# Soft-MoE tail of an attention kernel: the seventh w2 whole in two pieces, two output tiles in column halves, idle matmuls in the waits for w2, the last w1 pair in one transfer

## The chip, the core and the metric

The kernel runs on one NeuronCore of a Trainium2 chip. Its five engines (TensorE for matmuls, VectorE, ScalarE, GpSimd, SyncE) run from queues of their own, and 16 DMA engines move data between the device memory and the core's on-chip memory. The metric is the device time of one launch in microseconds (us); lower is better. The time before is 180.16 us, the median of three runs.

## The reference

Attention over 8 batches of 8 heads, 576 positions and 64 values each: heads 0 to 3 see a window of 32 positions back, heads 4 to 7 see every fourth of the last 128. The result, as 4608 rows of 512, goes through a mixture of experts with soft slots: every expert has four slots, each a weighted mean of all rows; an expert is two matrices with a ReLU between; every output row is a weighted mean of the 32 slots' results.

```python
def _attn_ref(q, k, v):                     # q, k, v: (8, 8, 576, 64) float32
    scores = scale * np.matmul(q, k.transpose(0, 1, 3, 2))
    mask_plain = (rel >= 0) & (rel < window)
    mask_dil = (rel >= 0) & (rel < window * dilation) & (rel % dilation == 0)
    scores = np.where(masks[None, :, :, :], scores, -1000000000.0)
    ...                                     # softmax over the last axis
    return np.matmul(attn, v)

def _moe_ref(x, phi, w1, w2):               # x (4608, 512), phi (512, 32)
    logits = x @ phi                        # w1 (8, 512, 1024), w2 (8, 1024, 512)
    ...                                     # d: softmax of logits over the rows
    slot_input = (d.T @ x).reshape(E, S_per_e, D)
    for e in range(E):
        h = np.maximum(slot_input[e] @ w1[e], 0.0)
        slot_out[e] = h @ w2[e]
    ...                                     # c: softmax of logits over the slots
    return c @ slot_out.reshape(n_slots, D)
```

## The kernel before

**Inputs.** All inputs but a few first pieces are loaded by GpSimd's DMA queue, which turns float32 into float16 on the way. The order of that queue is written out by hand: q, k and v of the eight batches (`load_batch`, L180), then the experts' weights (`load_w1` L280, `load_both_w2` L292, `load_half` L298, `load_w2` L305). The batches live in eight "homes" of 8192 float16 values per partition, two to a tile (`twos`); when a batch has been used, its home takes one expert's w1 (4096 values per partition) and w2 (4096 values, 8 chunks of 512 columns). So a weight load waits until the attention has read what lay there. Batches in `PAIRED` (2 to 7) load the dilated heads' q and k (`qd`, `kd`) for two batches at once; `qp`, `kp` are those of the plain heads, `vp`, `vd` the two halves of v, and `vt` its last 64 rows.

**Attention.** A loop over 30 of the 32 units (batch, pair of heads), L676 to L730, computes scores, exponentials, values, the transposed rows and the slot weights. ScalarE, VectorE and TensorE work through it in program order; the weight loads are issued from within it: after unit 6 and 14 the first four experts', after unit 22 w1 of experts 4 and 5 and w2 of expert 4, at unit 26 w1 of expert 6, and after the loop w1 of expert 7, then w2 of experts 5, 6 and 7. The zeroing of four small tiles `hTp` stands in GpSimd's queue at units 26 to 29.

**Experts.** `expert_in` (L794) multiplies the slots by w1 for a pair of experts, `expert_turn` (L809) transposes the result, `expert_out` (L823) multiplies by w2, one matmul per chunk, all into one PSUM tile `sop`. `expert_out(e, side, chs)` can do one column half of the 512 (`SIDES`) and some of the chunks. The last two w2 come in pieces, in this order: chunks 0 to 3 of w2(6), the left column half of its chunks 4 to 7, the left half of w2(7) in chunks 0 to 5 and 6 to 7 (`PIECES`), and then the right halves of the same.

**Output.** When `sop`'s left half is complete it is copied to `so` (L895, ScalarE for the left, VectorE for the right), and the first `FIRST_TILES` = 3 of nine output tiles of 512 rows are computed for the left columns: `finish_rows` (L857) does a matmul for each of a tile's four row groups (L865), and ScalarE (L869) and VectorE (L871) take turns in scaling the result into `ot`; `finish_half` (L875) stores them from SyncE's queue (L881), tile 0 in two pieces, the others in one. The same follows for the right half, and then the other six tiles are done over all 512 columns (`finish_whole` L883, stores at L887, as grouped in `TOGETHER`). `warm` (L466) issues matmuls whose results nobody reads; at the start there are 12 of them.

Of the kernel before, what the change touches and what calls it, by code (L numbers as in the profile page):

```python
# [7 lines left out]
FP32 = mybir.dt.float32  # L8
# [6 lines left out]
H = 8  # L15
S = 576
D = 64
# [6 lines left out]
E_EXP = 8  # L24
# [6 lines left out]
RP, NP = 6, 96  # L31
RD = 24
# [5 lines left out]
NV = 2  # L38
SIDES = ((0, DMODEL // 2), (DMODEL // 2, DMODEL))
PIECES = ((0, 6), (6, 8))  # L40
HALF = 4
FIRST_TILES = 3
PAIRED = (2, 4, 6)
TOGETHER = ((3,), (4, 5), (6,), (7,), (8,))


@with_exitstack
def kernel(
# [10 lines left out]
    nc = tc.nc  # L59
# [13 lines left out]
    first = {}  # L73
# [106 lines left out]
    def load_batch(b):  # L180
        if b == 6:
            twos.append(big.tile([128, 2, 8192], FP16, name="home6", tag="home6"))
            homes.extend(twos[3][:, i] for i in range(2))
        t = homes[b]
        parts = raws.setdefault(b, {})
        at = 0

        def load_v(nm, h0, n_h, r0, dst):
            n_p = dst.shape[0]
            dst = dst.rearrange("p (h x) -> p h x", h=n_h)  # L190
            nc.gpsimd.dma_start(  # L191
                out=dst,
                in_=v[b, h0 : h0 + n_h, r0 : r0 + 4 * n_p, :].rearrange(
                    "h (p r) d -> p h (r d)", r=4
                ),
            )
            parts[nm] = dst.rearrange("p h (r d) -> p h r d", r=4)

        for nm, ten, hs, rows in (
            ("qp", q, 0, RP), ("kp", k, 0, RP), ("qd", q, 4, RD), ("kd", k, 4, RD),  # L200
        ):
            g = 4 * S // (NP * rows)
            n = g * rows * D
            if nm in ("qd", "kd") and b & 6 in PAIRED:
                if b % 2 == 0:
                    both = twos[b // 2][0:NP, :, at : at + n]
                    nc.gpsimd.dma_start(
                        out=both,
                        in_=ten[b : b + 2, hs : hs + 4].rearrange("e h s d -> e (h s) d").rearrange(
                            "e (p r) d -> p e (r d)", r=rows  # L210
                        ),
                    )
                    for i in range(2):
                        raws.setdefault(b + i, {})[nm] = both[:, i : i + 1]
                at += n
                continue
            parts[nm] = t[0:NP, at : at + n].rearrange("p (g x) -> p g x", g=g)
            at += n
            src = ten[b, hs : hs + 4].rearrange("h s d -> (h s) d").rearrange(
                "(g p r) d -> p g (r d)", g=g, r=rows  # L220
            )
            if b == 0 and nm in first:
                t0 = side_by_side(nm[0], 0)
                nc.vector.tensor_copy(
                    out=t0.rearrange("p r (h d) -> p r h d", h=2),
                    in_=first[nm].rearrange("p h (r d) -> p r h d", d=D),
                )
                nc.gpsimd.dma_start(out=parts[nm][:, 2:4], in_=src[:, 2:4])
            else:
                nc.gpsimd.dma_start(out=parts[nm], in_=src)  # L230
            if nm == "kp":
                if b == 0:
                    head_v = t[:, 6144:7168].rearrange("p (h x) -> p h x", h=4)
                    parts["vp"] = head_v.rearrange("p h (r d) -> p h r d", r=4)
                elif b < 2:
                    load_v("vp", 0, 4, 0, t[:, 6144:7168])
                else:
                    load_v("v", 0, 8, 0, t[:, 6144:8192])
                    parts["vp"], parts["vd"] = parts["v"][:, 0:4], parts["v"][:, 4:8]
                load_v("vt", 0, 8, 512, t[96:112, 0:2048])  # L240
        if b < 2:
            load_v("vd", 4, 4, 0, t[:, 7168:8192])

    def cast_first_v():
# [50 lines left out]
            in_=moe_w2[e : e + 2].rearrange("e (p c) f -> p e (c f)", p=128),  # L295
        )

    def load_half(e, side):  # L298
        d0, d1 = SIDES[side]
        nc.gpsimd.dma_start(  # L300
            out=w_tiles[e][1][:, HALF:8, d0:d1],
            in_=moe_w2[e].rearrange("(p c) f -> p c f", p=128)[:, HALF:8, d0:d1],
        )

    def load_w2(e):  # L305
        w2t = w_tiles[e][1]
        w2_from = moe_w2[e].rearrange("(p c) f -> p c f", p=128)
        if e == E_EXP - 2:
            nc.gpsimd.dma_start(
                out=w2t[:, 0:HALF].rearrange("p c f -> p (c f)"),  # L310
                in_=w2_from[:, 0:HALF].rearrange("p c f -> p (c f)"),
            )
            load_half(e, 0)
            return
        if e < E_EXP - 2:
            nc.gpsimd.dma_start(
                out=w2t.rearrange("p c f -> p (c f)"), in_=w2_from.rearrange("p c f -> p (c f)")
            )
            return
        w2t = w_tiles[e][1] = w2t.rearrange("p c f -> p (c f)").rearrange("p (s c f) -> p s c f", s=2, c=8)  # L320
        for n, (d0, d1) in enumerate(SIDES):
            if n == 1:
                load_half(e - 1, 1)
            for c0, c1 in PIECES:
                nc.gpsimd.dma_start(out=w2t[:, n, c0:c1], in_=w2_from[:, c0:c1, d0:d1])

# [318 lines left out]
            )  # L645
        nc.vector.tensor_copy(out=phi4, in_=pp[:, :, None, :].broadcast_to([128, 4, 4, N_SLOTS]))

    warm(12, heat)
    ctx.enter_context(tc.manual_schedule(engines={mybir.EngineType.Pool}))
    for b in range(B):  # L650
        load_batch(b)
# [24 lines left out]
    for u in range(NU - 2):  # L676
        b, ph = divmod(u, 4)
        if ph == 0:
            st = scores(u + 1)
            softmax_parts(u + 1, st)  # L680
            if u:
                x_transposes(u - 1)
            values(u)
        elif ph == 1:
            st = scores(u + 1)
            if b + 1 < B:
                regroup(4 * b + 4)
            if b:
                front_logits(b - 1)
            if b + 1 < B:  # L690
                transposes(4 * b + 4)
            values(u)
            x_transposes(u - 1)
            softmax_parts(u + 1, st)
        elif ph == 2:
            st = scores(u + 1)
            values(u)
            if b + 1 < B:
                regroup(4 * b + 6)
            softmax_parts(u + 1, st)  # L700
            if b + 1 < B:
                dilated_transposes(b + 1, "k")
                dilated_transposes(b + 1, "q")
            if b:
                front_rows(b - 1)
            x_transposes(u - 1)
            if u == 2:
                nc.vector.tensor_copy(out=vd[1][:, 0, 0:1], in_=xs[0][:, 0, 2 * D : 2 * D + 1])
        else:
            st = scores(u + 1)  # L710
            if b:
                front_slots(b - 1)
            values(u)
            softmax_parts(u + 1, st)
            if b + 1 < B:
                select_v(b + 1)
                transposes(4 * b + 6)
            x_transposes(u - 1)
            if b + 1 < B:
                spread_v(b + 1)  # L720
        if u in (6, 14):
            load_w1(u // 4 - 1, 2)
            load_both_w2(u // 4 - 1)
        if u == 22:
            load_w1(4, 2)
            load_w2(4)
        if u == 26:
            load_w1(6)
        if 26 <= u:
            nc.gpsimd.memset(hTp[u - 26], 0.0)  # L730

    load_w1(E_EXP - 1)
    load_w2(E_EXP - 3)
    load_w2(E_EXP - 2)
    load_w2(E_EXP - 1)
# [87 lines left out]
    def expert_out(e, side=None, chs=range(8)):  # L823
        d0, d1 = (0, DMODEL) if side is None else SIDES[side]
        w2t = w_tiles[e][1][:, side] if e == E_EXP - 1 else w_tiles[e][1][:, :, d0:d1]
        for ch in chs:
# [7 lines left out]
                skip_group_check=True,  # L834
            )

    expert_in(0)
    expert_in(1)
    for pr in range(4):
        expert_turn(pr)  # L840
        if pr < 2:
            expert_in(pr + 2)
        if pr == 1:
            front_sums(B - 1, ring.tile([128, 11, N_SLOTS], FP32, name="sums", tag="ring"))
        if pr < 3:
            expert_out(2 * pr)
            expert_out(2 * pr + 1)
    expert_out(6, chs=range(HALF))

    so = keep.tile([128, DMODEL], FP16, name="so", tag="so")  # L850
    fours = [
# [23 lines left out]
    def finish_half(i, side):  # L875
        d0, d1 = SIDES[side]
        ot = ots[i].rearrange("p j d -> p (j d)").rearrange("p (s j d) -> p s j d", s=2, j=4)[:, side]
        rows = out[512 * i : 512 * i + 512, d0:d1].rearrange("(m j) d -> m j d", j=4)
        for j0, j1 in ((0, 2), (2, 4)) if i == 0 else ((0, 4),):
            finish_rows(i, ot, range(j0, j1), d0, d1)  # L880
            nc.sync.dma_start(out=rows[:, j0:j1], in_=ot[:, j0:j1])  # L881

# [7 lines left out]
        )  # L890

    for n, (d0, d1) in enumerate(SIDES):
        expert_out(E_EXP - 2, n, range(HALF, 8))
        expert_out(E_EXP - 1, n)
        (nc.scalar.copy if n == 0 else nc.vector.tensor_copy)(out=so[:, d0:d1], in_=sop[:, d0:d1])  # L895
        for i in range(FIRST_TILES):
            finish_half(i, n)
# [36 lines left out]
```

## Time and profile before

| | |
|---|---|
| median of the runs (lowest to highest) | 180.16 us (179.79 to 180.61) |
| the profiled execution's own time | 180.08 us |
| its span, first to last instruction | 177.9 us |
| TensorE, VectorE, ScalarE, GpSimd busy | 145.3, 120.3, 124.0, 43.2 us |
| mean granted TensorE clock | 0.889 |
| DMA: GpSimd's queue / SyncE's queue | 30.41 MB / 10.26 MB |
| read from device memory, written to it | 61.93 MB, 9.44 MB |

In the lines of the profile, PE is TensorE, DVE VectorE, ACT ScalarE, POOL GpSimd and SP SyncE; L828 is line 828 of the kernel. A line of a timeline has the start, the time from the first start to the last end of a group, the engine, the line, the operation, what it writes and reads, the count, and in brackets the idle time before it and what ended that. A line of a table by stretches has the stretch, its length, the busy time and number of instructions of TensorE's matmuls, its weight loads, VectorE, ScalarE and GpSimd, then the granted clock (1.00 is full speed), the share of the 16 DMA engines' time that transfers in flight took (above 1 where they overlap), and GB/s. GB/s counts bytes as written, so a load that turns float32 into float16 counts half of what it reads.

### The profile page before, as it was taken

To read this page: it belongs to the slowest core of one execution; us is meant where nothing else is said; L and a number is where in the kernel's file an instruction comes from. 1 tells how busy PE (TensorE), PEld (TensorE's weight loads), DVE (VectorE), ACT (ScalarE), POOL (GpSimd) and SP (SyncE) were. 2 spreads that over 40 slices of the span, in tenths; PEclk is the share of its full clock that TensorE was granted. 3 is DMA by queue.
4 is the path that set the end of the run, shared out by engine and by line. 5 is a ranking of instruction groups with operands and counts; after the bars stand their busy time and mean duration, and the time that the engine had idled before them with its cause. 6 is when DMAs were issued, how large, how long until landed. Compare 5 with 4: busy or idle time off the path is not lost.

```text
span 177.9 us, 5105 instructions
## 1 busy us (share of the span) xinstructions
PE 145.3 (82%) x2137; PEld 99.4 (56%) x2137; DVE 120.3 (68%) x337; ACT 124.0 (70%) x233; POOL 43.2 (24%) x68
## 2 busy tenths in 40 slices
PE   6589889899999999999999999977899833897200
PEld 2367576687676676776677676755763311453000
DVE  7959896987988888898798898587120100689400
ACT  2588899999998998998998999952304100699300
POOL 7756443334333441001000500700011100000000
PEclk9987999999999999999999999996558985569955
DMA  5999999999999999999999999999999999999996
GB/s 162 243 198 207 199 205 212 199 200 204 212 200 201 202 213 199 217 223 214 214 219 215 215 217 217 214 219 214 214 221 214 208 197 194 252 382 423 431 424 267
DMA packets 27094, 41.28 MB, mean 232 GB/s; under 512 B 1344, under 2 KB 22848, under 8 KB 24512
## 3 DMA queue, kind: packets, MB, share of 16 engines
q0 software_dynamic: 22080, 30.41, 96.1%
q1 hardware_dynamic: 4784, 10.26, 14.9%
q10 hardware_dynamic: 208, 0.29, 0.6%
q8 instruction: 16, 0.26, 0.5%
q14 instruction: 6, 0.05, 0.1%
HBM read 61.93 MB, written 9.44 MB: 401 GB/s over the span
## 4 chain that ended last, share of the span: by engine, by line
DMA 47%; PE 31%; ACT 6%; DVE 5%; issue 2%; POOL 1%; DVEq 0%; ACTq 0%; POOLq 0%
DMA home<-in_moe_w_dram 37%; DMA home<-in_k_dram 9%; PE o L496 6%; PE f L865 4%; PE s L391 3%; PE rgx L516 3%; PE sel L270 2%; PE sel L259 2%; ACT kTd L364 2%; PE rgq L351 2%; ACT pd L424 2%; PE rgk L351 2%; PE l L534 1%; DVE ot L871 1%; ACT ot L869 1%
## 5 line engine op out<-in xcount | busy, mean ns | idle before, releaser
L501 DVE TENSOR_TENSOR x<-o,rc 128x640 f16<-128x640 f32 x32 | 26.6, 831 | 0.2
L417 ACT ACTIVATE pr<-s 128x960 f16<-128x960 f32 (+1 forms) x32 | 25.2, 795 | 0.0
L424 ACT ACTIVATE pd<-s 128x640 f16<-128x640 f32 x32 | 22.3, 719 | 1.1 <-PE s L400 1.0
L871 DVE TENSOR_SCALAR ot<-f,rrow 128x256 f32<-128x256 f32 (+1 forms) x24 | 13.2, 613 | 7.8 <-PE f L865 7.8
L433 DVE TENSOR_TENSOR Pp<-pr,fixed 128x1280 f16<-128x1280 f16 (+1 forms) x32 | 15.4, 520 | 0.0
L496 PE MATMUL o<-vd,P 128*128 128x65 f16 x256 | 15.1, 197 | 0.2 <-DVE x L501 0.2
L191 POOL DMA_DIRECT2D home<-in_v_dram x17 | 12.0, 709 | 13.1 <-DMA home<-in_k_dram 6.1
L869 ACT ACTIVATE ot<-f,rrow 128x256 f32<-128x256 f32 (+1 forms) x24 | 12.7, 583 | 2.6 <-PE f L865 2.2
L496 PE MATMUL o<-vp,Pp 128*128 128x65 f16 x288 | 13.7, 197 | 1.0 <-DVE x L501 1.0
L516 PE MATMUL rgx<-fixed,x 128*128 128x128 f16 x155 | 14.0, 222 | 0.6 <-ACT qTd L364 0.4
L865 PE MATMUL f<-so,ET 128*128 128x256 f16 (+1 forms) x48 | 12.3, 411 | 2.2 <-ACT ot L869 1.1
L286 POOL DMA_DIRECT2D home<-in_moe_w_dram x5 | 3.2, 637 | 41.5 <-PE sel L270 38.0
L352 ACT COPY qT<-rgq 128x576 f16<-128x576 f16 x16 | 10.3, 645 | 4.0 <-PE rgq L351 3.9
L391 PE MATMUL s<-qT,kTp 64*128 64x160 f16 (+1 forms) x160 | 10.6, 224 | 2.9 <-ACT pd L424 1.9
L534 PE MATMUL l<-xT,phi 128*128 128x288 f16 x64 | 11.6, 307 | 1.6 <-DVE xT L526 1.6
L496 PEld LDWEIGHTS <-P 128*128 128x128 f16 x288 | 11.8, 99 | 1.8 <-DVE xT L526 0.2
L522 ACT COPY xT<-rgx 128x512 f16<-128x512 f16 x16 | 9.7, 605 | 4.3 <-PE rgx L516 4.3
L496 PEld LDWEIGHTS <-Pp 128*128 128x128 f16 x288 | 11.1, 99 | 2.4 <-DVE x L501 1.2
L363 PEld LDWEIGHTS <-home 96*128 96x128 f16 x192 | 10.5, 100 | 3.1 <-DMA home<-in_k_dram 1.0
L391 PE MATMUL s<-qTd,kTd 64*128 64x144 f16 x128 | 12.1, 230 | 0.0
L443 DVE TENSOR_TENSOR P<-pd,fixed 128x1024 f16<-128x1024 f16 x16 | 10.9, 681 | 1.8 <-ACT pd L424 1.8
L516 PEld LDWEIGHTS <-x 128*128 128x128 f16 x160 | 10.2, 98 | 3.1 <-DVE x L501 1.6
(136 smaller groups left out, 318.3 us busy)
## 6 DMA issues: line engine op xcount, KB each, us to landing
home<-in_moe_w_dram POOLq DMA_DIRECT2D x5, 2048.0 KB, 38.9
home<-in_moe_w_dram POOLq DMA_DIRECT2D x4, 1024.0 KB, 33.9
out_dram<-ot SPq DMA_DIRECT2D x4, 1024.0 KB, 8.5
home<-in_v_dram POOLq DMA_DIRECT2D x6, 512.0 KB, 14.3
home<-in_q_dram POOLq DMA_DIRECT2D x9, 288.0 KB, 12.9
home<-in_k_dram POOLq DMA_DIRECT2D x9, 288.0 KB, 13.4
out_dram<-ot SPq DMA_DIRECT2D x4, 512.0 KB, 3.6
out_dram<-ot SPq DMA_DIRECT2D x1, 2048.0 KB, 6.8
```

What stands on the lines that cost most here:

```text
L191: nc.gpsimd.dma_start(out=dst, in_=v[b, h0 : h0 + n_h, r0 : r0 + 4 * n_p, :].rearrange("h (p r) d -> p h (r d)", r=4),)
L391: nc.tensor.matmul(st[:, g, at : at + n], kT[64 * g : 64 * g + 64, k0 : k0 + 128], qT[64 * g : 64 * g + 64, q0 : q0 + n], start=True, stop ...
L417: nc.scalar.activation(out=(pr[:, :, 0 : 3 * QW], pr[:, :, 3 * QW :])[part], in_=st[:, :, 0 : (480, 224)[part]], func=AF.Exp, scale=SCALE,)
L424: nc.scalar.activation(out=pr[:, part].rearrange("p c e t -> p e c t"), in_=st[:, :, 0 : 2 * DW].rearrange("p e (c t) -> p e c t", c=2), f ...
L433: nc.vector.tensor_tensor(out=Pp[:, :, b0 : b0 + nb, 0:w], in0=pr[:, :, b0 * QW : b0 * QW + nb * w].rearrange("p h (t c) -> p h t c", c=w) ...
L496: nc.tensor.matmul(ot[:, h, blk], lhs, rhs, start=(n == 0), stop=(n == len(mms) - 1), skip_group_check=True)
L501: nc.vector.tensor_tensor(out=xs[b][:, :, 2 * D * hp : 2 * D * hp + 2 * D].rearrange("p t (h d) -> p h t d", h=2), in0=ot[:, :, :, 0:D], i ...
L516: nc.tensor.transpose(rg[:, 128 * blk : 128 * blk + 128], x[:, blk, hl : hl + 128], ident)
L534: nc.tensor.matmul(lp, phi4[:, kc].rearrange("p a s -> p (a s)"), xT[:, kc, 288 * c : 288 * c + 288], start=(kc == 0), stop=(kc == 3), ski ...
L865: nc.tensor.matmul(fp, ET[:, c0 : c0 + 127 * nj + 1 : nj], so[:, d0:d1], start=True, stop=True)
L869: nc.scalar.activation(out=ot[:, j], in_=fp, func=AF.Copy, scale=scale)
L871: nc.vector.tensor_scalar(out=ot[:, j], in0=fp, scalar1=scale, scalar2=None, op0=ALU.mult)
```

## The change

- w2 of expert 6 is loaded in two pieces, chunks 0 to 3 and 4 to 7, each over all 512 columns; `load_half` is gone. w2 of expert 7 keeps its four pieces, which now follow each other. `expert_out(6)` takes its chunks before the column halves begin.
- Idle matmuls of 512 columns into a PSUM tile `idle`: 2 before `expert_out(5)`, 4 before the first chunks of expert 6, 4 after chunks 0 to 3 and 4 after chunks 4 to 7 (`FILL`).
- `FIRST_TILES` goes from 3 to 2; tile 2 is done whole. Tile 0 is stored in three pieces on the left side (row groups 0, 1, and 2 with 3) and in two on the right.
- w1 of experts 6 and 7 is one transfer, issued after the loop.
- Batches 2 to 7 lie otherwise in their two homes, and v of batches 4 and 5, and of 6 and 7, is one transfer each.
- 9 matmuls at the start in place of 12.

```diff
@@ -38,10 +38,10 @@
 NV = 2
 SIDES = ((0, DMODEL // 2), (DMODEL // 2, DMODEL))
 PIECES = ((0, 6), (6, 8))
-HALF = 4
-FIRST_TILES = 3
+FILL = (2, 4, 4, 4)
+FIRST_TILES = 2
 PAIRED = (2, 4, 6)
-TOGETHER = ((3,), (4, 5), (6,), (7,), (8,))
+TOGETHER = ((2,), (3,), (4, 5), (6,), (7,), (8,))
 
 
 @with_exitstack
@@ in load_batch
-        at = 0
+        paired = b & 6 in PAIRED
+        flat = twos[b // 2].rearrange("p e x -> p (e x)")
+        n = S * 4 * D // NP
...
+        at = (10240 + 2 * n * (b % 2)) if paired else 0
+        for nm, ten in (("qp", q), ("kp", k)):
+            home = flat if paired else t
+            parts[nm] = home[0:NP, at : at + n].rearrange("p (g x) -> p g x", g=4)
...
+        if paired:
+            if b < 4:
+                load_v("v", 0, H, 0, t[:, 6144:8192] if b == 2 else t[:, 0:2048])
+            elif b % 2 == 0:
+                load_v("v", 0, 2 * H, 0, flat[:, 6144:10240])
+            load_v("vt", 0, H, 512, t[96:112, 2048:4096])
+            parts["vp"], parts["vd"] = parts["v"][:, 0:4], parts["v"][:, 4:8]
+        else:
+            load_v("vt", 0, H, 512, t[96:112, 0:2048])
+        for i, (nm, ten) in enumerate((("qd", q), ("kd", k))):
...
+            elif b % 2 == 0:
+                both = flat[0:NP, 2 * n * i : 2 * n * i + 2 * n].rearrange("p (e x) -> p e x", e=2)
...
@@ in the loaders of w2, and below
             in_=moe_w2[e : e + 2].rearrange("e (p c) f -> p e (c f)", p=128),
         )
 
-    def load_half(e, side):
-        d0, d1 = SIDES[side]
-        nc.gpsimd.dma_start(
-            out=w_tiles[e][1][:, HALF:8, d0:d1],
-            in_=moe_w2[e].rearrange("(p c) f -> p c f", p=128)[:, HALF:8, d0:d1],
-        )
-
     def load_w2(e):
         w2t = w_tiles[e][1]
         w2_from = moe_w2[e].rearrange("(p c) f -> p c f", p=128)
-        if e == E_EXP - 2:
-            nc.gpsimd.dma_start(
-                out=w2t[:, 0:HALF].rearrange("p c f -> p (c f)"),
-                in_=w2_from[:, 0:HALF].rearrange("p c f -> p (c f)"),
-            )
-            load_half(e, 0)
-            return
-        if e < E_EXP - 2:
-            nc.gpsimd.dma_start(
-                out=w2t.rearrange("p c f -> p (c f)"), in_=w2_from.rearrange("p c f -> p (c f)")
-            )
+        if e < E_EXP - 1:
+            step = 4 if e == E_EXP - 2 else 8
+            for c in range(0, 8, step):
+                nc.gpsimd.dma_start(
+                    out=w2t[:, c : c + step].rearrange("p c f -> p (c f)"),
+                    in_=w2_from[:, c : c + step].rearrange("p c f -> p (c f)"),
+                )
             return
         w2t = w_tiles[e][1] = w2t.rearrange("p c f -> p (c f)").rearrange("p (s c f) -> p s c f", s=2, c=8)
         for n, (d0, d1) in enumerate(SIDES):
-            if n == 1:
-                load_half(e - 1, 1)
             for c0, c1 in PIECES:
                 nc.gpsimd.dma_start(out=w2t[:, n, c0:c1], in_=w2_from[:, c0:c1, d0:d1])
 
@@ -645,7 +644,7 @@
             )
         nc.vector.tensor_copy(out=phi4, in_=pp[:, :, None, :].broadcast_to([128, 4, 4, N_SLOTS]))
 
-    warm(12, heat)
+    warm(9, heat)
     ctx.enter_context(tc.manual_schedule(engines={mybir.EngineType.Pool}))
     for b in range(B):
         load_batch(b)
@@ -724,12 +723,10 @@
         if u == 22:
             load_w1(4, 2)
             load_w2(4)
-        if u == 26:
-            load_w1(6)
         if 26 <= u:
             nc.gpsimd.memset(hTp[u - 26], 0.0)
 
-    load_w1(E_EXP - 1)
+    load_w1(E_EXP - 2, 2)
     load_w2(E_EXP - 3)
     load_w2(E_EXP - 2)
     load_w2(E_EXP - 1)
@@ -834,6 +831,7 @@
                 skip_group_check=True,
             )
 
+    idle = ring.tile([128, 512], FP32, name="idle", tag="ring")
     expert_in(0)
     expert_in(1)
     for pr in range(4):
@@ -844,8 +842,13 @@
             front_sums(B - 1, ring.tile([128, 11, N_SLOTS], FP32, name="sums", tag="ring"))
         if pr < 3:
             expert_out(2 * pr)
+            if pr == 2:
+                warm(FILL[0], xT[:, 0, 0:512], idle)
             expert_out(2 * pr + 1)
-    expert_out(6, chs=range(HALF))
+    warm(FILL[1], xT[:, 0, 0:512], idle)
+    for n in range(2):
+        expert_out(6, chs=range(4 * n, 4 * n + 4))
+        warm(FILL[2 + n], xT[:, 0, 0:512], idle)
 
     so = keep.tile([128, DMODEL], FP16, name="so", tag="so")
     fours = [
@@ -876,7 +879,7 @@
         d0, d1 = SIDES[side]
         ot = ots[i].rearrange("p j d -> p (j d)").rearrange("p (s j d) -> p s j d", s=2, j=4)[:, side]
         rows = out[512 * i : 512 * i + 512, d0:d1].rearrange("(m j) d -> m j d", j=4)
-        for j0, j1 in ((0, 2), (2, 4)) if i == 0 else ((0, 4),):
+        for j0, j1 in (((0, 1), (1, 2), (2, 4)), ((0, 2), (2, 4)))[side] if i == 0 else ((0, 4),):
             finish_rows(i, ot, range(j0, j1), d0, d1)
             nc.sync.dma_start(out=rows[:, j0:j1], in_=ot[:, j0:j1])
 
@@ -890,7 +893,6 @@
         )
 
     for n, (d0, d1) in enumerate(SIDES):
-        expert_out(E_EXP - 2, n, range(HALF, 8))
         expert_out(E_EXP - 1, n)
         (nc.scalar.copy if n == 0 else nc.vector.tensor_copy)(out=so[:, d0:d1], in_=sop[:, d0:d1])
         for i in range(FIRST_TILES):
```

More of the change, by code (lines that the diff above doesn't have):

```diff
@@ L192, in load_v @@
                 out=dst,
-                in_=v[b, h0 : h0 + n_h, r0 : r0 + 4 * n_p, :].rearrange(
-                    "h (p r) d -> p h (r d)", r=4
-                ),
-            )
[L197 to L206, printed above, removed]
-                    nc.gpsimd.dma_start(
[L208 to L211, printed above, removed]
-                    )
[L213 to L217, printed above, removed]
+                in_=v.rearrange("b h s d -> (b h) s d")[
+                    H * b + h0 : H * b + h0 + n_h, r0 : r0 + 4 * n_p, :
+                ].rearrange("h (p r) d -> p h (r d)", r=4),
+            )
+            got = dst.rearrange("p h (r d) -> p h r d", r=4)
+            if n_h <= H:
+                parts[nm] = got
+            else:
+                for i in range(2):
+                    raws.setdefault(b + i, {})[nm] = got[:, H * i : H * i + H]
+        at = (10240 + 2 * n * (b % 2)) if paired else 0
+        for nm, ten in (("qp", q), ("kp", k)):
+            home = flat if paired else t
+            parts[nm] = home[0:NP, at : at + n].rearrange("p (g x) -> p g x", g=4)
             at += n
-            src = ten[b, hs : hs + 4].rearrange("h s d -> (h s) d").rearrange(
-                "(g p r) d -> p g (r d)", g=g, r=rows
-            )
-            if b == 0 and nm in first:
+            src = ten[b, 0:4].rearrange("h s d -> (h s) d").rearrange("(g p r) d -> p g (r d)", g=4, r=RP)
+            if b == 0:
                 t0 = side_by_side(nm[0], 0)
@@ L230, in load_batch @@
                 nc.gpsimd.dma_start(out=parts[nm], in_=src)
[L231 to L241, printed above, removed]
+        if b == 0:
+            head_v = t[:, 6144:7168].rearrange("p (h x) -> p h x", h=4)
+            parts["vp"] = head_v.rearrange("p h (r d) -> p h r d", r=4)
+        elif not paired:
+            load_v("vp", 0, 4, 0, t[:, 6144:7168])
+        if paired:
[5 more added lines that the diff above has]
+            parts["vp"], parts["vd"] = parts["v"][:, 0:4], parts["v"][:, 4:8]
+        else:
+            load_v("vt", 0, H, 512, t[96:112, 0:2048])
+        for i, (nm, ten) in enumerate((("qd", q), ("kd", k))):
+            if not paired:
+                at = 3072 + n * i
+                parts[nm] = t[0:NP, at : at + n][:, None, :]
+                nc.gpsimd.dma_start(
+                    out=t[0:NP, at : at + n],
+                    in_=ten[b, 4:8].rearrange("h s d -> (h s) d").rearrange("(p r) d -> p (r d)", r=RD),
+                )
+            elif b % 2 == 0:
+                both = flat[0:NP, 2 * n * i : 2 * n * i + 2 * n].rearrange("p (e x) -> p e x", e=2)
+                nc.gpsimd.dma_start(
+                    out=both,
+                    in_=ten[b : b + 2, 4:8].rearrange("e h s d -> e (h s) d").rearrange(
+                        "e (p r) d -> p e (r d)", r=RD
+                    ),
+                )
+                for j in range(2):
+                    raws.setdefault(b + j, {})[nm] = both[:, j : j + 1]
+        if not paired:
             load_v("vd", 4, 4, 0, t[:, 7168:8192])
@@ L307, in load_w2 @@
         w2_from = moe_w2[e].rearrange("(p c) f -> p c f", p=128)
-        if e == E_EXP - 2:
-            nc.gpsimd.dma_start(
-                out=w2t[:, 0:HALF].rearrange("p c f -> p (c f)"),
-                in_=w2_from[:, 0:HALF].rearrange("p c f -> p (c f)"),
-            )
-            load_half(e, 0)
-            return
-        if e < E_EXP - 2:
-            nc.gpsimd.dma_start(
-                out=w2t.rearrange("p c f -> p (c f)"), in_=w2_from.rearrange("p c f -> p (c f)")
-            )
+        if e < E_EXP - 1:
+            step = 4 if e == E_EXP - 2 else 8
+            for c in range(0, 8, step):
+                nc.gpsimd.dma_start(
+                    out=w2t[:, c : c + step].rearrange("p c f -> p (c f)"),
+                    in_=w2_from[:, c : c + step].rearrange("p c f -> p (c f)"),
+                )
             return
```

## The prediction

> **What bounds the kernel now.** I read the page's slices first, to see which resource never rests.
>
> ```profile
> PEclk9987999999999999999999999996558985569955
> DMA  5999999999999999999999999999999999999996
> GB/s 162 243 198 207 199 205 212 199 200 204 212 200 201 202 213 199 217 223 214 214 219 215 215 217 217 214 219 214 214 221 214 208 197 194 252 382 423 431 424 267
> ```
>
> The 16 DMA engines are busy from the first slice to the last: loads at about 200 to 220 GB/s (as written, after the cast) until some 150 us, then stores at 380 to 430. Compute runs alongside, so the time is the load stream, the seam between loads and stores, and the store stream. The clock falls to half around the seam.
>
> Next, GpSimd's timeline: does the load queue ever run dry?
>
> ```profile
> 97.60 0.54 POOL L286 DMA_DIRECT2D home<-in_moe_w_dram  x1 [12.67 <-PE sel L270]
> 111.57 0.53 POOL L286 DMA_DIRECT2D home<-in_moe_w_dram  x1 [11.23 <-PE sel L270]
> 124.28 0.70 POOL L325 DMA_DIRECT2D home<-in_moe_w_dram  x1 [8.92 <-DMA home<-in_moe_w_dram]
> 139.00 0.70 POOL L325 DMA_DIRECT2D home<-in_moe_w_dram  x1 [4.00 <-DMA home<-in_moe_w_dram]
> ```
>
> It does not. The w1 loads wait at 97.60 and 111.57 for a batch's last value selection, but with more than ten microseconds of transfers in flight. The L325 waits end when the transfer eight places ahead lands, which gives landing times: w1(4,5) 124.2, w2(4) 129.1, w1(6) 134.1, w1(7) 138.9.
>
> Then TensorE's timeline, whose DMA waits show when each late piece is there.
>
> ```profile
> 143.63 0.62 PE L828 MATMUL sop<-home,hTp 128*32 128x512 f16 x8 [1.22 <-DMA home<-in_moe_w_dram]
> 146.14 0.62 PE L828 MATMUL sop<-home,hTp 128*32 128x512 f16 x4 [1.55 <-DMA home<-in_moe_w_dram]
> 147.46 0.41 PE L828 MATMUL sop<-home,hTp 128*32 128x256 f16 x4 [0.71 <-DMA home<-in_moe_w_dram]
> 149.41 1.07 PE L828 MATMUL sop<-home,hTp 128*32 128x256 f16 x8 [1.54 <-DMA home<-in_moe_w_dram]
> 150.09 0.40 PE L828 MATMUL sop<-home,hTp 128*32 128x256 f16 x2
> ```
>
> w2(5) is there at 143.63, w2(6) chunks 0-3 (512 KB) at 146.14, the left half of chunks 4-7 (256 KB) at 147.46, and w2(7)'s left half at 149.41 (384 KB) and 150.09 (128 KB). So 512 KB whole costs 2.51 us, 256 KB in half rows 1.32, 384 KB 1.95, 128 KB 0.68. The right halves (256+384+128 KB) follow: 150.09 + 3.95 = 154.04.
>
> Last, quarter-microsecond stretches across the seam, and SP's queue.
>
> ```profile
> 150.75:151.00 0.25, 0.05 (x1) 0.05 (x1) 0.00 (x0) 0.15 (x1) 0.00 (x0) 0.50 1.45 193
> 152.25:152.50 0.25, 0.25 (x3) 0.19 (x2) 0.25 (x2) 0.25 (x2) 0.00 (x0) 0.50 0.82 111
> 153.25:153.50 0.25, 0.25 (x2) 0.00 (x0) 0.25 (x2) 0.25 (x2) 0.00 (x0) 0.50 1.23 293
> 154.50:154.75 0.25, 0.05 (x2) 0.00 (x0) 0.10 (x1) 0.00 (x0) 0.00 (x0) 0.50 0.67 238
> 161.50:161.75 0.25, 0.00 (x0) 0.00 (x0) 0.25 (x1) 0.25 (x2) 0.00 (x0) 1.00 1.56 615
> 152.15 0.91 SPq L881 DMA_DIRECT2D out_dram<-ot  x2
> ```
>
> The last column is GB/s. Loads taper from 193 to 111 after 151.2 (some engines are done before others) and end near 152.9, where stores begin: the first is issued at 152.15 and its bytes flow 0.8 us later. Column-half stores run at about 384 GB/s until 161.45, whole tiles at 427 until 176.2. A dip at 154.50 is the third store (tile 1's whole half, issued at 153.41 after four evictions).
>
> I model it from T = 151.80, the end of the first eviction (ACT, 151.36 + 0.44). Tile 1's half is stored by 156.0 = T + 4.2, set by evictions and SP's issues; four half tiles remain (2.10 MB / 384 = 5.46), then six whole ones (6.29 MB / 427 = 14.73). 156.0 + 5.46 + 14.73 = 176.2: the span's stores as seen.
>
> **The change, part by part.** All sums are against the profiled execution's 180.08 us (span 177.9, 2.2 around it), 0.08 under the median of 180.16.
>
> *w2(6) whole.* Chunks 4-7 come as one 512 KB piece before w2(7)'s left half. By the rows the left side is complete at 146.14 + 2.51 + 1.95 + 0.68 = 151.28 instead of 150.09: **+1.19**. The right side ends at 154.04 - (2 x 1.32 - 2.51) = 153.91. Every store waits for the left side, so this is on the path. What covers it? The taper ends at 152.9, the first store would be issued past that, and nothing queued takes its place.
>
> *Idle matmuls.* They sit in DMA waits. At full clock one more N=512 costs 0.22 us (late output matmuls: three in 0.95, four in 1.17), at half 0.43: the pair before expert 5 ends near 142.9, before 143.63; the next four lie beside the wait for 146.14; the others end near 147.4 and 149.9, before 148.65 and 150.60. If the clock holds, two isolated matmuls on the way to the first store (0.40 and 0.37 now) get about 0.12 us shorter each, estimated from half clock doubling the streaming of 256 columns. Does it hold? Three 3.4 us stretches that end at a change or none:
>
> ```profile
> 141.83:145.24 3.41, 1.53 (x20) 0.64 (x21) 0.26 (x2) 0.00 (x0) 0.00 (x0) 1.00 1.13 202
> 118.00:121.40 3.40, 1.88 (x41) 1.70 (x41) 2.54 (x5) 1.49 (x4) 0.00 (x0) 0.99 1.06 222
> 158.89:162.30 3.41, 2.65 (x12) 1.24 (x11) 3.41 (x6) 3.32 (x7) 0.00 (x0) 1.00 1.11 410
> ```
>
> The first column behind the length is TensorE's busy time. The clock fell after 45% and 55% busy and stayed after 78%. With the fills a 2.5 us period holds 0.4 + 0.9 us, about 52%: nearest to the rows that fell. Bounds -0.25 to 0; I take **-0.12**. The Trainium skill ("TensorE: Matmul & The Clock Gate", Part 1) says that half rate returns only after an idle window of about 3.4 us; by it the fills would hold the clock and the whole sum would be +0.59. The trace differs: no stretch at 121.4 or 145.24 was idle, and the clock fell.
>
> *Two tiles in halves.* Tile 2 (1.05 MB) moves from 384 to 427 GB/s: 2.73 - 2.46 = **-0.27**. The first whole store comes earlier in exchange: 160.25 - 154.04 = 6.21 us after the right side now, less four halves (4 x 0.22), so about 159.2 at half clock and 158.4 at full. Its bytes start 0.8 later, by 160.0; the halves run until T' + 4.2 + 2.73 = 159.9 or so. No gap, but little margin.
>
> *Finer first stores.* One row group is stored at a time for tile 0. Each issue takes SP about 0.4 us, so the four left stores are issued at T' + 0.14, 0.55, 1.0 and 1.6; tile 1's store still needs its evictions and stays at T + 4.2: 0. At best the bytes flow without a gap from T' + 1.0 (2.73 us): -0.46.
>
> *Merged loads.* Batches 5 and 7 bring no v of their own, w1(6,7) is one transfer. 512 KB took 2.51 us, half of w2(5)'s 4.87 is 2.44: 0.07 per transfer; w1(4,5), a pair, took 9.9, two singles 9.7: no gain. Between 0 and -0.28; **-0.08**.
>
> *Costs at nothing.* Three warm matmuls fewer (about 0.4 each), the new raw layout, and batch 4's qd and kd behind 512 KB more of v (2.5 us): hidden, since the experts start at 131.9 and run until they wait for weights at 138.76 and 143.63 (1.22). Without this cover each would shift the experts by its size. w1(6) is no longer issued at 97.60 but with w1(7) at about 112; w2(5) to w2(7) stand behind it on GpSimd's queue as they do now, the zeroing of hTp comes earlier, and w2(4) in flight until 129.1 covers 17 us. SP keeps 13 stores.
>
> Sum: 1.19 - 0.12 - 0.27 - 0.08 = **+0.72**: 180.80 by the profiled execution, 180.9 by the median.
>
> **Rivals.** *Slower: the clock falls inside the fills.* If it is at half from about 148.65, chunks 4-7 take 0.62 and four fills 4 x 0.43 = 1.7: TensorE is free at 150.97, past the landing at 150.60, which costs about 0.15. Whole-tile matmuls then also pace the first whole store (0.3 gap). 1.19 + 0.15 - 0.27 + 0.3 = +1.37: 181.5. For it: the 52%. Against: fills use the whole array, the rows that fell did not. It decides when the clock is at half from 148.65 on. Chance 0.40.
>
> *Not slower: the loads end more evenly.* The taper loses (193 - 112)/193 x 1.75 = 0.73 us. If half-row packets cause it, a third fewer of them plus the full 0.28 of merging and the gapless 0.46 give 0.72 + 0.08 - 0.24 - 0.28 - 0.46 = -0.18: 180.0; with the whole taper gone -0.67: 179.5. Against it: the half rows that remain come last. Chance 0.14.
>
> *A fixed price per transfer.* 2 x 1.32 - 2.51 = 0.13 is the most that rows give; four transfers fewer by this are -0.52, so +0.28: 180.4. Chance 0.08. The Trainium skill ("DMA: Bandwidth & Descriptors", Anatomy of one DMA) fits 2.0 us fixed to each, which would be 8 us here, an estimate of 172; the 2.51 us for 512 KB in flight speaks against it, as that price is latency.
>
> **How the numbers follow.** The forecast case has 0.38. A measurement here tells about 0.5%, 0.9 us: faster is below 179.3, slower above 181.1. The slower rival lies mostly beyond (0.35 of 0.40), the forecast sometimes (0.08); the taper rival reaches faster in most of its upper end, with what I don't see: 0.12. Slower 0.43, same 0.45. Range 179.6 to 181.8: from the taper rival to 0.3 past the slow one.
>
> **What would show it.** TensorE's first wait for w2(7)'s left half should end near 150.6 and 151.3; SP's first store at 152.9 (now 152.15); a hole in the DMA share near 153; stores ending near 176.9. The clock from 145 to 159 tells which bound holds. A first store before 152.2, or loads that end before 152, would prove me wrong.

## The result, and the profile after

The changed kernel takes 180.39 us (median), the one before 179.90 in the same comparison: a ratio of 1.0031, with a 95% interval of 1.0019 to 1.0044. That is 0.5 us more; the forecast was 0.72 (180.9 against 180.16). Sign and size came out. Of the terms behind them, some did not, and three effects that stood in no term turned up on the way. The trace below is of an execution that took 182.06 us; its span, 178.42, is like that of the other runs (178.1 to 178.8), so its excess lies outside the span.

The page's slices of the changed kernel (clock, DMA share, GB/s):

```profile
PEclk9999999999999999999999999998556999999755
DMA  5999999999999999999999999999999999799996
GB/s 152 245 200 205 201 202 215 199 201 200 207 208 201 199 211 205 225 209 220 219 209 222 217 209 220 217 215 217 215 220 213 210 205 184 191 408 424 428 430 276
```

The DMA engines are now below 90% busy in one slice in the middle, the 35th (151.6 to 156.1 us), where 252 GB/s have become 191. The clock is full from 137 us to the end of the output matmuls; before, it was at half from 145 to 159. TensorE's timeline:

```profile
146.35 0.40 PE L825 MATMUL sop<-home,hTp 128*32 128x512 f16 x4 [0.69 <-DMA home<-in_moe_w_dram]
148.79 0.40 PE L825 MATMUL sop<-home,hTp 128*32 128x512 f16 x4 [1.06 <-DMA home<-in_moe_w_dram]
150.74 0.40 PE L825 MATMUL sop<-home,hTp 128*32 128x256 f16 x6 [0.59 <-DMA home<-in_moe_w_dram]
151.42 0.29 PE L825 MATMUL sop<-home,hTp 128*32 128x256 f16 x2 [0.28 <-DMA home<-in_moe_w_dram]
```

The pieces arrive 2.44, 1.95 and 0.68 us apart, and the left side is complete at 151.42 (forecast 151.28, before 150.09). The last matmuls take 0.29 where they took 0.40. Then SyncE's first store, and stretches across the seam (the last three columns are clock, DMA share and GB/s):

```profile
152.98 0.36 SPq L884 DMA_DIRECT2D out_dram<-ot  x1
153.25:153.50 0.25, 0.16 (x6) 0.11 (x6) 0.25 (x2) 0.25 (x2) 0.00 (x0) 1.00 0.37 47
153.50:153.75 0.25, 0.25 (x6) 0.10 (x6) 0.25 (x1) 0.25 (x2) 0.00 (x0) 1.00 0.10 12
154.75:155.00 0.25, 0.00 (x0) 0.00 (x0) 0.21 (x1) 0.00 (x0) 0.00 (x0) 1.00 0.43 152
155.50:155.75 0.25, 0.25 (x4) 0.21 (x2) 0.25 (x1) 0.25 (x2) 0.00 (x0) 1.00 0.51 172
160.50:160.75 0.25, 0.00 (x0) 0.00 (x0) 0.25 (x1) 0.25 (x1) 0.00 (x0) 1.00 0.70 295
163.50:163.75 0.25, 0.07 (x1) 0.00 (x0) 0.25 (x2) 0.25 (x2) 0.00 (x0) 1.00 0.70 295
163.75:164.00 0.25, 0.23 (x2) 0.13 (x2) 0.25 (x1) 0.25 (x1) 0.00 (x0) 1.00 1.24 524
```

The first store goes out at 152.98 (152.15 before). Near 153.5 next to nothing moves, and between the small first stores there are gaps (154.75, 155.50). The 295 GB/s at 160.50, just behind the half tiles, are no gap: the stream of whole tiles swings between 295 and 524 later too (163.50, 163.75).

The trace also has, for each transfer, the times at which the 16 DMA engines raise its completion counter, each when its own share is done. For the last load and the last store (the first, eighth and sixteenth engine to be done, us):

```
            last load                 last store
before      151.25  153.19  154.11    176.59  176.67  177.00
after       151.12  152.88  154.10    177.28  177.35  177.50
f3 (below)  151.28  152.98  154.14    176.35  176.51  177.09
f1 (below)  151.17  152.87  153.88    177.17  177.24  178.97
```

The engines end the loads almost 3 us apart; the "taper" is this. From the last engine's end of the loads to the last engine's end of the stores it is 22.89 us before and 23.40 after. The counters do not say which engine raised them, so that these are the same engine is not shown.

### The profile page after: what moved, and what is told of

It reads as the page before. It is cut to its first block, busy times and chain, and to the rows that moved or that the text cites. A ratio compares the mean times of both kernels' runs of the same rounds, so it can differ in the third digit from the quotient of the medians.

```text
span 178.4 us, 5102 instructions
## 1 busy us (share of the span) xinstructions
PE 147.5 (83%) x2140; PEld 100.1 (56%) x2140; DVE 119.6 (67%) x335; ACT 122.9 (69%) x231; POOL 40.0 (22%) x64
## 4 chain that ended last, share of the span: by engine, by line
PE 46%; DVE 19%; DMA 14%; ACT 9%; issue 4%; POOL 0%; DVEq 0%; POOLq 0%; ACTq 0%
DMA home<-in_moe_w_dram 14%; PE o L495 12%; DVE ot L874 6%; PE s L390 5%; PE sel L282 4%; PE rgx L515 4%; PE sel L271 4%; ACT pd L423 3%; PE rgq L350 3%; PE rgk L350 3%; ACT kTd L363 3%; DVE P L442 3%; PE l L533 2%; PE u L596 2%; DVE rc L499 2%
## 5 line engine op out<-in xcount | busy, mean ns | idle before, releaser
L874 DVE TENSOR_SCALAR ot<-f,rrow 128x512 f32<-128x512 f32 (+1 forms) x22 | 12.5, 645 | 8.0 <-PE f L868 8.0
L872 ACT ACTIVATE ot<-f,rrow 128x512 f32<-128x512 f32 (+1 forms) x22 | 11.6, 628 | 2.0 <-PE f L868 1.7
L193 POOL DMA_DIRECT2D home<-in_v_dram x15 | 10.7, 715 | 8.8 <-DMA home<-in_k_dram 4.2
L868 PE MATMUL f<-so,ET 128*128 128x512 f16 (+1 forms) x44 | 10.3, 340 | 2.4 <-ACT ot L872 1.2
L362 PEld LDWEIGHTS <-home 96*128 96x128 f16 x192 | 10.6, 102 | 3.0 <-issue 0.8
```

The costliest lines, as they stand in the source:

```text
L872: nc.scalar.activation(out=ot[:, j], in_=fp, func=AF.Copy, scale=scale)
L874: nc.vector.tensor_scalar(out=ot[:, j], in0=fp, scalar1=scale, scalar2=None, op0=ALU.mult)
```

## The experiments: undoing the order and the fills

All times below are medians, with the kernel before at 179.83 to 179.85 in the same runs.

**e1, the old order of w2(6) with two half tiles**

```diff
+        if e == E_EXP - 2:
...
+            load_half(e, 0)
+            return
...
+            if n == 1:
+                load_half(e - 1, 1)
...
-    for n in range(2):
-        expert_out(6, chs=range(4 * n, 4 * n + 4))
-        warm(FILL[2 + n], xT[:, 0, 0:512], idle)
+    expert_out(6, chs=range(HALF))
+    warm(FILL[2], xT[:, 0, 0:512], idle)
...
+        expert_out(E_EXP - 2, n, range(HALF, 8))
+        if n == 0:
+            warm(FILL[3], xT[:, 0, 0:512], idle)
```

(The three dots stand for lines left out.) `load_half` and its order are those of the kernel before; the last four idle matmuls ("fills") now stand behind the left half of chunks 4 to 7.

> The changed kernel with one part undone: w2(6) chunks 4 to 7 come in column halves again, in the order of before; two tiles in halves, fills and the rest stay. My theory (every store waits for the left side; the left side is 1.2 to 1.3 us earlier by the old order, but two half tiles are too few to bridge to the right side): left side complete near 150.1, stores of the left side done near 155.7, first right store's bytes near 156.7, so a hole of about 1 us moves behind the left stores; stores end near 176.5, about 0.3 above before and 0.3 below the changed kernel, some 180.1 to 180.2 where before is 179.9. Rival (the order alone costs 1.2 us, and nothing takes its place): 179.2, clearly faster than before.

**e2, the same with three half tiles** (`FIRST_TILES = 3`, tile 2 out of `TOGETHER`)

> As the one before, and with three tiles in halves again: what is left of the change are the fills, the finer first stores, the merged loads and the layout. My theory: left side at 150.1, clock full, first eviction done 1.44 us after it (now 1.71), no hole before the right stores, so before less the 0.27 of the clock: 179.6 where before is 179.9. Rival A (the clock buys nothing, since the DMA engines are the bound): 179.9. Rival B (merged loads shorten the stream too): 179.3.

**e3, no fills** (`FILL = (0, 0, 0, 0)`)

> The changed kernel without any idle matmul. My theory: the clock falls near 145 to 149 and stays at half until the output is under way; the first eviction ends 0.27 us later after the left side, and the stores end 0.3 us later: 180.7 where the changed kernel has 180.4. Rival (the clock is off the path): 180.4, no difference. Rival (whole-tile matmuls at half clock also starve the first whole store): 181.0.

**e4, three half tiles in the new order**

> The changed kernel with three tiles in column halves. My theory: the hole at the seam is unchanged, and 1.05 MB more go out at 384 in place of 427 GB/s: 0.27 us more, 180.7. Rival (half rows cost nothing at the end, or a hole behind two tiles goes away): 180.4 or less.

Measured: e1 182.55, e2 181.39, e3 181.19, e4 182.29. In e3 the clock fell (half from 151.0 to 157.8) and the time rose by 0.8, more than the 0.3 of my theory and near the number of the rival that starves the first whole store (181.0). The stretch without fills is 20% busy, and the first whole-tile store is issued at 159.34 where the changed kernel has 158.51.

```profile
147.40:150.80 3.40, 0.67 (x10) 0.22 (x10) 0.00 (x0) 0.00 (x0) 0.00 (x0) 1.00 1.40 194
159.34 0.34 SPq L890 DMA_DIRECT2D out_dram<-ot  x1
```

Neither theory nor rival has the whole way. The first store is no later (152.97 against 152.98). At the eighth engine the last half tile lands 0.34 us later (160.54 against 160.20), and only 0.10 comes on top at the first whole tile (2.58 us behind it against 2.48). This execution, 180.94, is the fastest of its five and shows about half of the 0.8.

The other three are 1.6 to 2.4 us off, and neither theory nor rival foresaw it. In their traces one engine runs on alone for 1.2 to 1.7 us behind the fifteenth. In e2 and e4 the others are not far off: the eighth ends at 176.69 (176.67 before) and 177.53 (177.35 in the changed kernel). In e1 all are late besides: the eighth ends at 178.19, where 176.5 was expected. And the table of DMA queues has one transfer more in the queue for instructions. The trace's list of packets shows what that queue does: a 16 KB transfer starts at about every 256th instruction of TensorE, sixteen times in the kernel before, the last at 142.5. The changed kernel has a seventeenth only at 180.85, after the end of its span. In e1, e2 and e4, which have 4 to 8 more matmuls than the changed kernel, a seventeenth starts at 166.0, 161.9 and 165.1, amid the stores.

## The experiments: the length of TensorE's program

**f1, four matmuls more at the very start**

```diff
-    warm(9, heat)
+    warm(13, heat)
```

> The changed kernel with 13 instead of 9 warm matmuls at its very start, where TensorE waits anyway; nothing else. In the traces so far a 16 KB instruction transfer starts at about every 256th TensorE instruction; the kernels with 8 to 16 more TensorE instructions than the changed one had a seventeenth of them at 161.9, 165.1 and 166.0 us, amid the stores, and one of the 16 DMA engines was 1.2 to 1.7 us late from there to the end. New theory (the length of TensorE's program decides): these four matmuls, 150 us before the end, make the kernel 1.2 to 1.7 us slower: 181.6 to 182.1, with a seventeenth transfer in the store stream. Rival (what was slow in those kernels lay in their load order and tiles): 180.4, no difference.

Measured: 182.04, ratio to before 1.0124 (1.0106 to 1.0141), or 1.65 us above the changed kernel. The instruction queue of the changed kernel and of f1 in their tables, and the end of f1:

```profile
q8 instruction: 16, 0.26, 0.5%
```

```profile
q8 instruction: 17, 0.28, 0.6%
177.00:177.50 0.50, 0.00 (x0) 0.00 (x0) 0.00 (x0) 0.00 (x0) 0.00 (x0) 0.50 0.08 33
177.50:178.00 0.50, 0.00 (x0) 0.00 (x0) 0.00 (x0) 0.00 (x0) 0.00 (x0) 0.50 0.08 33
```

A share of 0.08 is little more than one engine of 16. In the table of counters above, f1's eighth engine ends at 177.24, its last at 178.97. Four matmuls in a wait 150 us before the end cost 1.65 us, because they bring the seventeenth instruction transfer (at 165.02) into the store stream. So the "three warm matmuls fewer" of the change, which I had put down as hidden, matter: with 9 of them the seventeenth transfer stays out of the stores, with 13 it does not. 12, the number of the kernel before, were not tried with the fills.

The next three repeat e1, e2 and e4 with fewer warm matmuls (3, 1 and 3; f3 also has none before expert 5), so that the program is about as long as before.

**f2, old order, two half tiles**

> The changed kernel with the old order of w2(6) and w2(7), as before, but with 3 warm matmuls at the start so that TensorE's program is no longer than before. New theory: the seventeenth instruction transfer goes and 1.5 to 1.7 us with it: about 180.9; what is left over the changed kernel is the hole behind two half tiles. My first theory said 180.1 to 180.2. Rival (the old order itself is slow with two tiles): 182.5 as it was.

**f3, old order, three half tiles**

> Old order and three tiles in halves, with one warm matmul at the start and none before expert 5, so that TensorE's program is no longer than before. New theory: 181.4 less 1.2 for the late engine: 180.0 to 180.2, about the kernel before. My first theory (the clock's 0.27 on top): 179.6. Rival (merged loads or finer stores are what was slow): 181.4 as it was.

**f4, new order, three half tiles**

> The changed kernel with three tiles in halves, with 3 warm matmuls at the start. New theory: 182.3 less 1.5 for the late engine: 180.8, or 0.1 to 0.4 above the changed kernel, which is the price of half rows for the third tile (0.27 in my sum). Rival (three tiles are slow by themselves): 182.3 as it was.

Measured: f2 180.63, f3 180.18, f4 180.62; the seventeenth transfer is gone in all three, as the new theory said. f2 shows the hole that the first theory put behind two early half tiles. This execution took 181.26, 0.6 above the median, and its clock is at half from 153.7 to 160.5, so the order alone may not account for the hole's size:

```profile
156.00:156.50 0.50, 0.50 (x5) 0.33 (x3) 0.50 (x2) 0.50 (x3) 0.00 (x0) 0.50 0.40 139
156.50:157.00 0.50, 0.50 (x4) 0.37 (x3) 0.50 (x2) 0.50 (x3) 0.00 (x0) 0.50 0.02 6
```

f3 is a puzzle: its last store lands at 177.09, as before (177.00), yet it took 0.33 more. The difference is behind the last landing. SyncE ends with eight waits, one for each counter that its stores take in turn. f3 has 14 stores, the kernel before and the changed one 13.

## The experiments: the last waits, and what is left

**g1, f3 with 13 stores** (tile 0's left side in two pieces, as before)

```diff
-        for j0, j1 in (((0, 1), (1, 2), (2, 4)), ((0, 2), (2, 4)))[side] if i == 0 else ((0, 4),):
+        for j0, j1 in ((0, 2), (2, 4)) if i == 0 else ((0, 4),):
```

> The old order, three tiles and shortened TensorE program of the run that gave 180.18, with tile 0's left side stored in two pieces as before, so 13 stores in place of 14. Theory: with 14 stores the last one lies in the lane that SyncE waits for first at the end, and seven waits of 0.062 us each follow its landing (177.11 to 177.54 in that trace); with 13 it lies in the last lane. So 0.43 less: 179.7 to 179.8, level with the kernel before or 0.1 under it; what is left of the change there (clock, merged loads) buys next to nothing, because the slowest DMA engine ends its loads at the same time. My sum had -0.20 for these: 179.65. Rival (merged loads or layout cost 0.3): 180.1 to 180.2.

**g2, the kernel before with 14 stores** (that line the other way round)

> The kernel before with one edit: tile 0's left side stored in three pieces (row groups 0, 1, and 2 with 3), so 14 stores. Theory of the last waits: last landing as before, near 177.0, and 0.43 us more behind it: 180.3. Rival (finer first stores start the store stream earlier and cost nothing): 179.85 or less.

Measured: g1 179.75, ratio to before 0.9998 (0.9987 to 1.0009); g2 180.47, ratio 1.0031 (1.0020 to 1.0042). SyncE's waits for landed stores at the end (total, how many, longest), before and in g2:

```profile
SPq L929 <- DMA out_dram<-ot: 9.4, 4, 2.4
```

```profile
SPq L929 <- DMA out_dram<-ot: 10.6, 1, 10.6
```

With 13 stores the last counter in the row is the last to fill, so the waits are worked off as stores land. With 14 it is the first in the row: one wait of 10.6 us, and seven more behind it, at 177.13 to 177.50 in g2's trace, 0.062 apart. That is 0.43 of the 0.64 by which g2 is slower. Its last landing (177.05) is as before, and the median span of its runs is 0.45 longer (178.45 against 178.0), so inside the span the waits are the whole difference; the other 0.2 lies outside it, where two of g2's six runs have 2.2 and 2.3 us in place of 1.8. The finer first stores brought nothing here. Two more pairs agree: from f3 to g1 and from f4 to g4 the fourteenth store goes and 0.43 and 0.45 us with it.

**g3, the changed kernel with the left side of both half tiles in two pieces**

```diff
+        for j0, j1 in ((0, 2), (2, 4)) if i == 0 or side == 0 else ((0, 4),):
```

> The changed kernel with the left side of both half tiles stored in two pieces of two row groups each; 13 stores as in it. In its trace the first 2.2 us of stores (153.75 to 156.0) lose some 0.55 us to gaps between small stores and before tile 1's single one. Theory (supply of stores bounds there): gaps shrink and the end comes about 0.35 earlier: 180.0 to 180.1. Rival (other waits, on the right side, take it back): 180.4, no difference.

Measured: 180.34, ratio to before 1.0037 (1.0020 to 1.0055), no different from the changed kernel by the time. The rival holds in the main: from 154.0 the stores flow without a gap, but then they wait for the right side (311 GB/s), and the last landing is 0.17 earlier (177.33 against 177.50) in place of 0.35:

```profile
154.50:155.00 0.50, 0.15 (x2) 0.15 (x3) 0.29 (x1) 0.00 (x0) 0.00 (x0) 1.00 1.09 383
156.50:157.00 0.50, 0.50 (x4) 0.28 (x3) 0.50 (x3) 0.50 (x2) 0.00 (x0) 1.00 0.89 311
```

**g4, the new order with three half tiles and 13 stores**

> The changed kernel with three tiles in halves, a program for TensorE no longer than before, and tile 0's left side in two pieces, so 13 stores; it had 180.62 with 14. Theory of the last waits: 180.2, that is 0.2 under the changed kernel, so two tiles in place of three bought nothing here (my sum had -0.27), since the first whole tile comes too late behind two half tiles. Rival (the third half tile costs its 0.27): 180.6.

Measured: 180.17, ratio 1.0019 (1.0010 to 1.0029), as the theory of the last waits said. But its reason, that the first whole tile comes too late behind two half tiles, is not in the traces. At the eighth engine the first whole tile lands 2.48 us behind the last half tile in g4 (162.76, 165.23) and in the changed kernel (160.20, 162.68), and the stores of the changed kernel end 0.10 earlier (177.35 against 177.45). What is longer in the changed kernel is the time outside the span. Each run has its time and its span (listed to 0.1 us); medians of the span, and of the time less the span:

| half tiles | kernels | span | time less span |
|---|---|---|---|
| three | before | 178.0 | 1.83 |
| three | e2, e4, f3, f4 | 179.6, 180.45, 178.4, 178.8 | 1.79, 1.81, 1.79, 1.79 |
| three | g1, g2, g4 | 177.95, 178.45, 178.4 | 1.81, 1.83, 1.77 |
| two | changed kernel | 178.3 | 2.12 |
| two | e1, e3, f1, f2, g3 | 180.45, 179.1, 179.95, 178.5, 178.2 | 2.10, 2.10, 2.12, 2.13, 2.12 |

Every kernel with two half tiles pays some 0.3 us outside the span, every one with three does not. e4 differs from the changed kernel by the third half tile alone. What these 0.3 us are no trace here shows.

No version here beats both kernels by more than its interval; g1 is level with the one before.

## Why the prediction came out, point by point

| step | forecast | measured | by |
|---|---|---|---|
| w2(6) whole, left side later | +1.19 | +0.42 | g4 - g1 (180.17 - 179.75); f4 - f3 gives +0.44 |
| third tile whole (with finer stores) | -0.27 | -0.1 in the span | after - g4, spans |
| time outside the span | 0 | +0.35 | after - g4 (2.12 - 1.77) |
| clock and merged loads, old order | -0.20 | -0.08, interval -0.23 to +0.16 | g1 - before |
| sum | +0.72 | +0.56 | |

Rows two and three together are +0.22 (180.39 - 180.17; spans are listed to 0.1 us), and the intervals of the two ratios overlap. The sum counts against the last round's kernel before; in its own comparison it is +0.49. The differences pair g1 and g4 also with their numbers of warm matmuls and the fill before expert 5. Four warm matmuls more moved fifteen of 16 engines by about 0.1 us at the end (f1 against the changed kernel), so little is expected of that.

That the sum came out near is luck in part: one term was 0.77 too high, and 0.35 us that stood in no term took half of it back.

**What was right.** The time is loads, seam and stores. The left side is complete 1.33 us later in the trace (1.19 by the rows of before), the first store 0.83 later (forecast 152.9, seen 152.98), the DMA engines have a hole at 153.5, the stores land 0.5 to 0.7 us later. The third tile's step (below) held inside the span.

**The term that was mis-sized: w2(6) whole.** The step said that every store waits for the left side, so the delay is on the path, and that nothing covers it. The delay is there, its price is 0.42 and not 1.19. The cover is the taper: the last load packets start at 153.78 before and 153.77 after, not near 152.9 as I read from the average rate, so the slowest engines are still loading in either order. f4 and f3, both with 14 stores and three half tiles, show it engine by engine: by the new order the first engine ends its stores 1.03 us later (177.38 against 176.35), near the forecast, the eighth 0.96, the last 0.45 (177.54 against 177.09), and the last one is waited for. f3 against before shows it from the other side: its stores start at 151.78 in place of 152.15, its fastest engine ends 0.24 earlier (176.35), its slowest 0.09 later (177.09). An average rate over 16 engines hid that. Why the last engine still pays 0.45 is not shown.

**The third tile, and a term that was missing.** "No gap, but little margin" held: the half tiles are followed by the first whole one without loss (2.48 us in both kernels). The price of half rows was right too: in g4 half tiles land 1.33 to 1.37 us apart and whole ones 2.43 to 2.48, so two halves take 0.2 to 0.3 us more than a whole (forecast 0.27). Inside the span two half tiles are 0.1 us faster than three (178.3 against 178.4; 0.2 for g3), the way that was forecast and less. What the prediction left out is the time around the span, which it took as fixed (2.2 in its execution of the kernel before, 1.83 at the median). With two half tiles it is 2.12, and that takes back more than the third tile gives. Its cause stays open.

**The clock.** The fills held it, against my reading of the rows (52% busy, nearest to those that fell). What a full clock is worth depends on the order. In the old one g1 cannot tell it from nothing, nor from the forecast (interval -0.23 to +0.16). In the new order with two half tiles it is worth 0.8 (e3 against after, by the time and by the median span, 179.1 against 178.3), where I had 0.25 at most: at half clock the half tiles come late as well as the first whole one. The rival "the clock falls inside the fills" had a price near that (+1.37 against e3's 1.3 over before), but its condition did not occur, and some 0.3 of e3's 1.3 are the time outside the span.

**Costs at nothing.** Batches' layout, order of qd and kd, the w1 pair: g1 has them all and is level with before. The number of warm matmuls does not come for nothing: it decides on 1.65 us. The Trainium skill ("DMA: Bandwidth & Descriptors", Anatomy of one DMA) has 2.0 us fixed for each transfer. That price is not seen here: g1 has three loads fewer and is level with before.

## What to carry to other kernels

Where DMA bounds the kernel, read the engines one by one at a seam: the last one to end is waited for, and starting the others earlier buys less than it moves them (0.45 of 1.03 us here). Before adding idle instructions, count the engine's instructions: a further block of them comes by DMA, and here it cost 1.65 us amid the stores. A variant that changes the number of stores can change the last waits too; compare the last landing and the span, not only the time.

## What the runs showed of the hardware

- TensorE's instructions come in 16 KB transfers, one per some 256 instructions. With one in the store stream one of 16 engines ended 1.2 to 1.7 us after the others (e1, e2, e4, f1), though the transfer itself is listed with 0.95. Why the delay is longer than the transfer stays open.
- Waits on counters that are already full took SyncE 0.062 us each, one after the other (177.13 to 177.50 in g2).
- TensorE's clock stayed full over a stretch that was 52% busy with 512-column matmuls, six of ten on the full array (147.30 to 150.71 in the changed kernel) and fell after one that was 55% busy with small ones (118.00 to 121.40 before). The share of busy time alone does not tell; that the small ones count for less is my inference, which no run here isolates.

```profile
147.30:150.71 3.41, 1.79 (x10) 0.59 (x9) 0.00 (x0) 0.00 (x0) 0.00 (x0) 1.00 1.39 193
```

- The 16 DMA engines end the load stream almost 3 us apart (151.25 to 154.11 before). Why some lag stays open.
